# One kernel, one edit: the folded output weight as three rounded products, the sum of keys spread by two transfers, and the first attention tiles in another order

## The chip, the core and the metric

The kernel runs on one core of a Trainium2 chip. The core has engines that run side by side and meet at semaphores: TensorE (PE in the profile: matrix products and transposes), VectorE (DVE), ScalarE (ACT), GpSimd (POOL), and SyncE (SP), which here does nothing but issue the DMA transfers between device memory (DRAM) and on-chip memory (SBUF). Products end in accumulator banks (PSUM). Each engine runs its instructions in the order in which they were written down. The metric is device time in microseconds (us) of one execution; lower is better.

## The reference, cut to what matters

```python
x = A_x                                  # 2048 x 576
xn = _layernorm(x)
q, k, v = xn @ wqkv                      # 32 heads of 18
pq, pk = phi(q), phi(k)                  # phi(t) = (t + 1 if t > 0 else exp(t)) + 1e-6
kv = einsum("bhsd,bhse->bhde", pk, v)    # one 18 x 18 block a head
z = sum of pk over the tokens            # 576 numbers: the sum of keys
o = (pq @ kv) / (pq . z + 1e-6)
s = o @ wo
g = _silu(gelu(xn @ w1 + b1) @ w2 + b2)  # 576 -> 4608 -> 576
out = x + s * g
```

All inputs and the output are float32.

## The kernel before, in words

**Numbers in two halves.** TensorE takes two kinds of operand here: plain float32 (`F32`) and rounded float32 (`F32R`). Where the kernel uses the rounded kind it writes an operand `a` as `hi + lo`: `hi` is a rounded copy of `a`, made on ACT, and `lo` is `a - hi`, made on DVE (lines with `op=SUB`). A product is then three rounded products, hi*hi + hi*lo + lo*hi. The two halves of a weight are the tiles that end in `h` and `l`.

**Stages.** Tokens lie in 16 tiles of 128. Phase 1 goes through pairs of tiles. For each pair a Winograd-like scheme computes queries, keys and values (`products`, with steps 2, 1, e2, sa, 6, sb, e5, 7, 5, 4, 3 from `ORDER_X`; a number is a product with the weight pair `W_OF[number]`, and e2 and e5 are products with the last 64 rows of the weight). The accumulator banks `x0`, `xa` and `x1` hold three running results; `snapshot` (L900) copies `xa` to SBUF between products, since later sums need it as it stood. After each step a hook of the caller runs, and this is where everything else is put: the order of the whole phase is this hand-written order, engine by engine. Steps sa and sb are `state` (L473): 10 products that add the pair before to `ps_kva` and `ps_kvb`, the matrices kv of all heads with the sum of keys as one more row (row 126, `G`). The first two pairs are computed by `plain_x` without that scheme (L390 from `x00` to `x11`), and the first `state` stands between `x10` and `x12`.

For the last two pairs (tiles 12 to 15) the keys and values come first (part "kv"), and the queries after them (part "q"), once for pair 6 and once for pair 7. The hooks of these two query passes hold the end of the attention's preparation:

- `masked_state` copies the sum of keys out of PSUM (L1077, L1078) and the blocks on the diagonal of kv into `kvz` (`copy_predicated`, L1079 to L1081).
- `make_zb` spreads the sum of keys over all 128 partitions: a product with a matrix whose last row is ones (L1128), and a copy (L1132).
- `fold_wo` multiplies kv with the output weight: kw = kvz x wo, five groups of heads in six steps of two products (L1152), each copied from PSUM by ACT (L1159) or DVE (L1157), and moved to rows of another tile by DMA (L1163 to L1167). All of these products are plain float32.
- `by_sums` (POOL, L1101) multiplies phi(q) with the spread sum of keys, `denominators` (DVE, L1108 to L1112) adds up each head and inverts, `p_mult` (POOL, L1116) divides phi(q), and `pad` (ACT, L1123) fills the last columns.
- `split_kw` (ACT L1193, DVE or POOL L1194) makes the two halves of kw, and `store_kw` (L1197) stores it for later.

**The ten attention tiles.** `TO` lists ten of the tiles. For each, `transpose_p` turns phi(q) over on TensorE (5 transposes into `ptp`, L1252) and writes its halves `th` (ACT, L1256) and `tl` (DVE, L1257, L1258); `attend` multiplies them with kw into `ps_s` (28 products, L1287), copies the result (L1296) and stores it. While tile j is multiplied, tile j+2 is transposed and the sums of tiles j+4 and j+5 are made. `beside` puts other preparation for the feed-forward network between these tiles; among it is a sum of three terms on DVE (`sum_rest`, L534 to L538).

**The rest.** The feed-forward network follows (L1575, L1741), with the six other attention tiles spread through its second half. It takes four fifths of the time.

**Transfers.** All are issued by SP in the order of the program; each also waits until the one eight before it has landed.

Of the kernel before, what the change touches and what calls it, by code (L numbers as in the profile page):

```python
# [15 lines left out]
P = 128  # L16
# [31 lines left out]
def linear_attention_gated_ffn(ctx, tc, x, xT, wqkv, wo, w1, w1e, b1, w2, b2, out):  # L48
# [64 lines left out]
    zb_dram = dram.tile([P, D], F32, name="zb_dram")  # L113
# [51 lines left out]
    ORDER_X = (2, 1, "e2", "sa", 6, "sb", "e5", 7, 5, 4, 3)  # L165

# [19 lines left out]
    def q_tile(t):  # L186
        q_of[t] = tq.tile([P, D], F32, tag="q", name=f"q{t}", bufs=4)
# [237 lines left out]
    def phi_hi(key, src):  # L425

        e = e_of[key] = tq.tile([P, D], F32, tag="e", name=f"e{key}")
        nc.scalar.activation(as2(e), src, AF.Relu, scale=-1.0)
        nc.scalar.activation(e, e, AF.Exp, scale=-1.0)
        nc.scalar.activation(e, e, AF.Identity, bias=tiny[:, 0:1])  # L430

# [385 lines left out]
    k10 = phi_plain(2, x10)  # L817
    state(0)
    x12 = bank2("x12")
    plain_x(1, 1, 0, x12, THEN)  # L820
# [34 lines left out]
    def late_tiles(p):  # L855
        r_tile(p)
        f = R[p].rearrange("p a b -> p (a b)")
        if p == NPR:
            at = 0
            for n, cols in (("kvz", 640), ("sums_k", D), ("last_row", P), ("zb", D), ("mf", G)):  # L860
                late[n] = f[:, at : at + cols]
                at += cols
# [12 lines left out]
    def make_mask():  # L875
# [3 lines left out]
        nc.gpsimd.memset(late["sums_k"], 0.0)  # L879
        nc.gpsimd.memset(late["last_row"], 0.0)  # L880
        nc.gpsimd.affine_select(
            out=late["last_row"], in_=late["last_row"], compare_op=ALU.not_equal, fill=1.0,
            base=-G, pattern=[[0, P]], channel_multiplier=1,
        )
# [17 lines left out]
    def products(p, part, hooks, before=None):  # L902
# [8 lines left out]
        for i in ORDER_X:  # L911
# [57 lines left out]
    def phase1_pair(p):  # L969
# [8 lines left out]
        def h2():  # L978
# [7 lines left out]
            for n, t in enumerate(qp[::-1]):  # L986
                phi_q_hi(t)
# [3 lines left out]
        def h1():  # L991
            if early:
                rest_hi(prep), x_hi_ops(prep, 0, 14)
            for t in qp[::-1]:
                phi_q_max(t), store_q(t)
# [64 lines left out]
    for p in range(2, NPR):  # L1060
# [5 lines left out]
        2 * NPR - 3, 2 * NPR - 4, 2 * QH, 2 * QH + 1, 2 * NPR - 2, 2 * QH + 2, 2 * NPR - 1,  # L1066
# [3 lines left out]
    kvz, sums_k, last_row, zb_first = (late[n] for n in ("kvz", "sums_k", "last_row", "zb"))  # L1070
    wo_sb = late["wo"] + [k_bufs[0]]
    ln = GROUPS[-1][1]

    def masked_state():
        mask = late["mask"]
        nc.sync.dma_start(wo_sb[4][: GROUPS[4][1]], wo[GROUPS[4][0] :, :])
        nc.scalar.copy(sums_k[96 : G + 1, : 4 * G], ps_kv[0][96 : G + 1, : 4 * G])  # L1077
        nc.scalar.copy(sums_k[96 : G + 1, 4 * G :], ps_kv[1][96 : G + 1, :ln])  # L1078
# [4 lines left out]
    def first_phi():  # L1083
        phi_q_hi(TO[0]), phi_q_max(TO[0])
# [1150 lines left out]
```

## Time and profile before

| | us |
|---|---|
| Median of three runs (1088.2 to 1089.11) | 1088.75 |
| The profiled execution | 1088.02 |
| Its span, from first to last instruction | 1086.1 |
| PE busy in the span | 1075.6 (99%) |
| DVE, ACT, POOL busy | 819.6, 524.4, 535.2 |
| Query pass of pair 6 begins | 176.65 |
| First product of the spread and the fold (zb) | 187.43 |
| First transposes of the attention tiles | 202.36 |
| First product of the first attention tile | 203.85 |
| Feed-forward network begins | 247.49 |

The table gives the profiled execution's own time beside its span: 1.9 us lie outside the span, and the median of the runs lies 0.73 us above the profiled execution. Starts are counted from the span's start. A row of the timeline reads: start, duration, engine, line, operation, output and inputs, for products the size of the array's part and of the output, count, and in brackets the idle time of the engine just before and what ended it. The duration of one product includes its way through the array, so the distance between the starts of neighbouring products tells what one costs.

### The profile page before, as it was taken

Reading aid. Unit: us, or ns where it says so; the run is one execution under the profiler, and the core shown is the slowest. Engines: PE = TensorE matmul, PEld = TensorE weight load, DVE = VectorE, ACT = ScalarE, POOL = GpSimd, SP = SyncE. Lnnn points to the kernel's source line nnn. Section 1 sums busy time; section 2 is a strip of 40 time slices with the busy share of each in tenths; the row PEclk is TensorE's granted clock in tenths of the full one; section 3 lists DMA queues with packets and bytes.
Section 4 is the critical chain, followed back from the end, with each engine's and each line's share of the span. In section 5 each row is a group of like instructions: output and inputs, shape, how many; then the busy total and the mean of one; then the engine's idle time right before and its main releaser. Section 6 shows DMA issues by size and latency. Waiting matters only on the chain.

```text
span 1086.1 us, 17916 instructions
## 1 busy us (share of the span) xinstructions
PE 1075.6 (99%) x6492; PEld 990.6 (91%) x6492; DVE 819.6 (75%) x1197; ACT 524.4 (48%) x872; POOL 535.2 (49%) x555
## 2 busy tenths in 40 slices
PE   9999999999999999999999999999999999999998
PEld 8999999898988989989899898998989899998988
DVE  7997853787898988989889886575847566574856
ACT  7656655645454554544545445253443444242442
POOL 3133141576596776866867754143433525242340
PEclk9999999999999999999999999999999999999999
DMA  6678634699567585685765797886767657666653
GB/s 240 195 290 226 219 127 147 224 378 378 195 248 274 215 299 202 226 302 197 288 245 205 267 393 288 288 302 216 224 198 238 213 180 244 201 228 226 215 156 130
DMA packets 91120, 258.63 MB, mean 238 GB/s; under 512 B 12182, under 2 KB 25494, under 8 KB 88728
## 3 DMA queue, kind: packets, MB, share of 16 engines
q1 hardware_dynamic: 91032, 257.49, 68.8%
q8 instruction: 51, 0.84, 0.3%
q14 instruction: 37, 0.30, 0.1%
HBM read 155.16 MB, written 101.40 MB: 236 GB/s over the span
## 4 chain that ended last, share of the span: by engine, by line
PE 94%; ACT 2%; DMA 1%; DVE 1%; issue 1%; POOL 1%; SPq 0%; POOLq 0%; ACTq 0%; DVEq 0%
PE pm L1741 35%; PE a L1575 11%; PE zy L1575 11%; PE e L1575 11%; PE b L1575 5%; PE xaall L390 4%; PE x L390 3%; PE pd L1862 2%; PE x1all L390 2%; PE psa L1287 2%; PE ps_s L1287 1%; PE ps_kva L473 1%; PE x0all L390 1%; PE xakv L390 1%; DMA s_dram<-s 1%
## 5 line engine op out<-in xcount | busy, mean ns | idle before, releaser
L1678 POOL TENSOR_TENSOR g<-g 128x256 f32<-128x256 f32 x204 | 185.6, 938 | 56.5 <-DVE h_l L1329 49.5
L1747 DVE TENSOR_TENSOR macc<-pm,macc 128x576 f32<-128x576 f32 x218 | 163.9, 752 | 44.0 <-PE pm L1741 43.1
L1326 ACT CAST h_h<-g 128x512 fp32r<-128x512 f32 x204 | 122.7, 621 | 117.4 <-PE pm L1741 116.4
L1329 DVE TENSOR_TENSOR h_l<-g,h_h 128x512 fp32r<-128x512 f32 x204 | 165.2, 816 | 2.3 <-ACT h_h L1326 2.3
L1575 PE MATMUL a<-X,wa 128*128 128x512 f32 x432 | 110.1, 390 | 0.0
L1575 PEld LDWEIGHTS a<-X,wa 128*128 128x128 f32 x432 | 79.7, 188 | 15.3
L1592 ACT COPY mid<-a 128x512 f32<-128x512 f32 x36 | 21.1, 585 | 111.2 <-PE a L1575 111.2
L1678 POOL TENSOR_TENSOR mid<-g 128x256 f32<-128x256 f32 x68 | 52.0, 784 | 45.6 <-ACT g L1583 44.5
L1595 DVE TENSOR_TENSOR mid<-b,mid 128x512 f32<-128x512 f32 x36 | 24.8, 689 | 61.4 <-PE b L1575 61.3
L1377 POOL TENSOR_TENSOR w1raw<-w1raw 128x256 f32<-128x256 f32 x18 | 13.3, 740 | 90.6 <-ACT h_h L1326 47.7
L1583 ACT ACTIVATE g<-b,b1c 128x512 f32<-128x512 f32 x36 | 24.8, 689 | 66.9 <-DVE b L1601 66.8
L1575 PE MATMUL e<-X,wc 128*128 128x512 f32 x216 | 55.4, 392 | 0.0
L1575 PE MATMUL zy<-X,wd 128*128 128x512 f32 x216 | 54.9, 389 | 0.0
L1575 PE MATMUL e<-X,wd 128*128 128x512 f32 x216 | 54.8, 389 | 0.0
L1575 PE MATMUL zy<-X,wc 128*128 128x512 f32 x216 | 54.8, 389 | 0.0
L274 POOL TENSOR_TENSOR R<-R,bc 128x640 f32<-128x640 f32 x9 | 15.8, 1770 | 70.4 <-DMA R<-xT 47.1
L1575 PEld LDWEIGHTS zy<-X,wd 128*128 128x128 f32 x216 | 40.5, 188 | 8.6
L1575 PEld LDWEIGHTS zy<-X,wc 128*128 128x128 f32 x216 | 40.5, 188 | 8.4
L1575 PEld LDWEIGHTS e<-X,wd 128*128 128x128 f32 x216 | 40.5, 188 | 8.4
L1575 PEld LDWEIGHTS e<-X,wc 128*128 128x128 f32 x216 | 40.1, 188 | 8.1
L1583 ACT ACTIVATE g<-e,b1c 128x512 f32<-128x512 f32 x36 | 24.8, 689 | 45.3 <-DVE e L1608 45.3
L1994 POOL TENSOR_TENSOR qa<-qa,dena 128x576 f32<-128x576 f32 x6 | 7.0, 1168 | 62.5 <-issue 56.6
(1019 smaller groups left out, 3234.6 us busy)
## 6 DMA issues: line engine op xcount, KB each, us to landing
we<-we_dram SPq DMA_DIRECT2D x72, 224.0 KB
w2raw<-w SPq DMA_DIRECT2D x10, 1152.0 KB
x_dram<-X SPq DMA_DIRECT2D x6, 1792.0 KB
w1raw<-w SPq DMA_DIRECT2D x18, 512.0 KB
op_a<-wa SPq DMA_DIRECT2D x18, 512.0 KB
op_c<-wc SPq DMA_DIRECT2D x18, 512.0 KB
op_d<-wd SPq DMA_DIRECT2D x18, 512.0 KB
wc<-op_c SPq DMA_DIRECT2D x18, 512.0 KB
```

What stands on the lines that cost most here:

```text
L390: nc.tensor.matmul(dst, st, w, start=start, stop=stop, skip_group_check=True)
L1287: nc.tensor.matmul(ps[:, h, :HD], st[:, k, :], w[v][k][:, h * HD : (h + 1) * HD], start=(i == 0), stop=(i == len(seq) - 1),)
L1326: nc.scalar.copy(pair[0], src)
L1329: eng.tensor_tensor(pair[1], src, pair[0].bitcast(F32), op=SUB)
L1575: nc.tensor.matmul(ps, st, mv, start=first and n == 0, stop=n == len(seq) - 1, skip_group_check=True,)
L1583: nc.scalar.activation(g, ps, AF.Gelu_apprx_tanh, bias=b1c[:, f : f + 1])
L1592: nc.scalar.copy(m1_sb, A)
L1595: tt(u1_sb, B, m1_sb, op=ADD)
L1678: nc.gpsimd.tensor_tensor(dst[:, cs], a[:, cs], b[:, cs], op=op)
L1741: nc.tensor.matmul(ps[:, q, :HD], hs[p][st][:, cs], m[:, p, :], start=(n == 0 and i not in CHAIN), stop=(n == 5), skip_group_check=True,)
L1747: nc.vector.tensor_tensor(dst, src, dst, op=ADD)
L1862: nc.tensor.matmul(ps, st[:, cs], w_all.rearrange("p n d -> p (n d)")[:, w], start=(i == 0), stop=(i == len(seq) - 1),)
```

## The change

- **Fold.** The weights of the fold are split: `wo_hi` and `wo_lo` write the halves of the five pieces of wo into places of weight tiles whose key and value columns are no longer needed (`kv_columns` of T2, T3, T4), and `state_hi` and `state_lo` write the halves of kvz. Each product of the fold becomes three rounded ones. The last groups are copied from PSUM by ACT alone. The fold begins after step 1 of the last query pass, where it began after step 2.
- **Sum of keys.** `make_zb` goes. The row is stored to DRAM (`z_dram`, 576 numbers) and loaded again into all 128 partitions (`sum_of_keys`). The later copy for the second half is loaded from the same row, and the store of the whole spread tile goes.
- **Order.** Tiles 8 and 9 become the first attention tiles; their queries are loaded into the places of wo (`load_early_q`). In both query passes e2 comes before product 1 (`ORDER_Q`). The first transposes come before step 3 of the last query pass. Sums on POOL, `split_kw`, the third step of `sum_rest` and the first `state` change places; within an attention tile the 28 products go through `th` with the high half, `tl`, and `th` with the low half.

On PE at the end of phase 1 (`x0q`, `xaq` and `x1q` are the banks of the last query pass, `ps_kw` those of the fold), before:

```order
L390 MATMUL x0q_1974<-wB21h,X 128x288
L1128 MATMUL zb_1981<-R_1542 128x288
L1128 MATMUL zb_1984<-R_1542 128x288
L1152 MATMUL ps_kw_1989<-R_1718,R_1542 126x288
L1152 MATMUL ps_kw_1992<-R_1718,R_1542 126x288
L390 MATMUL xaq_1995<-wB11h,X 128x288
L390 MATMUL xaq_1995<-wB11l,X 128x288
L390 MATMUL xaq_1995<-wB11h,X 128x288 x2
```

On PE at the same place, now:

```order
L392 MATMUL x0q_1988<-wRh,XR_1571 128x288
L392 MATMUL x0q_1988<-wRl,XR_1571 128x288
L392 MATMUL xaq_1999<-wB11h,X 128x288
L392 MATMUL xaq_1999<-wB11l,X 128x288
L392 MATMUL xaq_1999<-wB11h,X 128x288 x2
L392 MATMUL xaq_1999<-wB11l,X 128x288
L392 MATMUL xaq_1999<-wB11h,X 128x288
L1201 MATMUL ps_kw_2009<-X,wT4h 126x288 x2
L1201 MATMUL ps_kw_2009<-X,wT4l 126x288
L1201 MATMUL ps_kw_2014<-X,wT4h 126x288 x2
L1201 MATMUL ps_kw_2014<-X,wT4l 126x288
```

The two products of the spread are gone, the fold stands behind product 1, and one product of it is three.

On SP from the end of the state to the fold's first moves (`kph` and `R` take the last piece of wo, `weo` are halves of another weight, `zb` is the spread sum, `b1c` a bias), before:

```order
L1076 DMA kph_134<-wo 72x576
L592 DMA we_dram<-weo_1926 128x1792
L1092 DMA b1c<-b 128x36
L1163 DMA kw_1987<-kw_1987 2x576
L1166 DMA kr_2012<-kw_1987 112x576
```

On SP at the same place, now:

```order
L1104 DMA R_1542<-wo 72x576
L1119 DMA z_dram<-R_1542 1x576
L1114 DMA zb<-z_dram 128x576
L1101 DMA R_1713<-q_dram 128x576 x2
L601 DMA we_dram<-weo_1908 128x1792
L1149 DMA b1c<-b 128x36
L1212 DMA kw_2007<-kw_2007 2x576
```

The store of the row, the load that spreads it and two loads of queries now stand ahead of the store of `weo` and of the fold's moves.

On DVE in the middle of the attention tiles (`wa_rest0ef` is the sum of three terms), before:

```order
L536 SCALAR_TENSOR_TENSOR wa_rest0ef<-wa_rest0gm,sgn,wa_rest0ef 64x512
L538 TENSOR_TENSOR wa_rest0ef<-wa_rest0ef,wa_rest0gm 32x512
L1257 TENSOR_TENSOR tl_2485<-ptp_2478,th_2484 128x512
L1258 TENSOR_TENSOR th_2484<-ptp_2478,th_2484 64x128
L1108 TENSOR_REDUCE den_2492<-bs_2437 128x32
```

On DVE at the same place, now:

```order
L545 SCALAR_TENSOR_TENSOR wa_rest0ef<-wa_rest0gm,sgn,wa_rest0ef 64x512
L1322 TENSOR_TENSOR tl_2509<-ptp_2502,th_2508 128x512
L1323 TENSOR_TENSOR th_2508<-ptp_2502,th_2508 64x128
L547 TENSOR_TENSOR wa_rest0ef<-wa_rest0ef,wa_rest0gm 32x512
L1165 TENSOR_REDUCE den_2517<-bs_2462 128x32
```

The third step of the sum has moved behind the halves of a transposed tile.

The diff, cut to its core:

```diff
-    zb_dram = dram.tile([P, D], F32, name="zb_dram")
+    z_dram = dram.tile([1, D], F32, name="z_dram")
...
     ORDER_X = (2, 1, "e2", "sa", 6, "sb", "e5", 7, 5, 4, 3)
+    ORDER_Q = (2, "e2", 1, "sa", 6, "sb", "e5", 7, 5, 4, 3)
...
-    state(0)
     x12 = bank2("x12")
-    plain_x(1, 1, 0, x12, THEN)
+    plain_x(1, 1, 0, x12, THEN[:6], last=False)
+    state(0)
+    plain_x(1, 1, 0, x12, THEN[6:], first=False)
...
             if p == NPR - 2:
-                rest_lo(prep), x_lo_ops(prep, 0, 8), x_lo_ops(prep, 8, 14)
+                x_lo_ops(prep, 8, 14), rest_lo(prep), x_lo_ops(prep, 0, 8)
...
     TO = [
-        2 * NPR - 3, 2 * NPR - 4, 2 * QH, 2 * QH + 1, 2 * NPR - 2, 2 * QH + 2, 2 * NPR - 1,
+        2 * QH, 2 * QH + 1, 2 * NPR - 3, 2 * NPR - 4, 2 * NPR - 2, 2 * QH + 2, 2 * NPR - 1,
...
+    def wo_hi(i):
+        nc.scalar.copy(wo_ops[i][0], wo_src[i])
+
+    def wo_lo(i):
+        h, l = wo_ops[i]
+        nc.vector.tensor_tensor(l, wo_src[i], h.bitcast(F32), op=SUB)
+
+    def sum_of_keys(dst):
+        nc.sync.dma_start(dst, bass.AP(tensor=z_dram.tensor, offset=z_dram.offset, ap=[[0, P], [1, D]]))
+
+    def state_sums():
+        nc.scalar.copy(sums_k[96 : G + 1, : 4 * G], ps_kv[0][96 : G + 1, : 4 * G])
+        nc.scalar.copy(sums_k[96 : G + 1, 4 * G :], ps_kv[1][96 : G + 1, :ln])
+        nc.sync.dma_start(z_dram, sums_k[G : G + 1])
+        zb.append(tw.tile([P, D], F32, tag="raw", name="zb", bufs=1))
+        sum_of_keys(zb[0])
...
     products(NPR - 2, "q", {
-        1: round_sums, "sb": lambda: (masked_state(), round_hi()), 7: lambda: (round_lo(), round_store()),
-        4: first_phi,
+        2: load_last_wo,
+        "e2": lambda: (round_sums(), wo_hi(0), wo_hi(1), wo_lo(0), wo_lo(1)),
+        "sa": lambda: (round_hi(), round_lo(), wo_hi(2), wo_lo(2)),
+        "sb": state_sums,
+        "e5": lambda: (masked_state(), load_early_q(0), load_early_q(1), wo_hi(3)),
+        7: lambda: (state_hi(), wo_hi(4), wo_lo(3)),
+        5: lambda: (state_lo(), wo_lo(4), round_store()),
+        4: lambda: phi_q_hi(TO[2]),
     }, NPR - 1)
...
-                nc.tensor.matmul(
-                    ps, kvz[:rows, at : at + n], wo_sb[i][:rows, hs], start=True, stop=True
-                )
+                for m, (v, w) in enumerate(((0, 0), (0, 1), (1, 0))):
+                    nc.tensor.matmul(
+                        ps, kvz_at(v, rows, at, n), wo_ops[i][w][:, h], start=m == 0, stop=m == 2
+                    )
                 dst = kw[i][:n, hs] if n < P else kr4[:, hs]
-                if h:
+                if h and i < 3:
                     nc.vector.tensor_copy(dst, ps)
...
-    products(NPR - 1, "q", {2: f2, 1: f1, 6: f6, 7: f7, 5: f5, 4: f4})
+    products(NPR - 1, "q", {
+        2: f2, 1: f1, "sa": fsa, 6: f6, "e5": fe5, 7: f7, 5: f5, 4: f4,
+    })
...
-        seq = []
-        for k in range(4):
-            seq += [(th, 0, k), (th, 1, k), (tl, 0, k)]
+        seq = [(st, v, k) for st, v in ((th, 0), (tl, 0), (th, 1)) for k in range(4)]
         seq += [(th, 0, 4), (th, 1, 4)]
...
-        1: ((0, "split", 0),), 2: ((0, "sums", 0),), 3: ((0, "sums", 1), (0, "sums", 2)),
+        1: ((0, "split", 0),), 2: ((0, "sums", 0),), 3: ((0, "sums", 1),),
...
+        if j == 4:
+            rests[0].sums(2)
...
-        if 0 < j < NA - 5:
+        if 1 < j < NA - 5:
             by_sums(j + 5)
         if j + 4 < NA:
             denominators(j + 4)
             p_mult(j + 4)
+        if j < 2:
+            by_sums(j + 5)
```

More of the change, by code (lines that the diff above doesn't have):

```diff
@@ L993, in h1 @@
                 rest_hi(prep), x_hi_ops(prep, 0, 14)
-            for t in qp[::-1]:
+            for n, t in enumerate(qp[::-1]):
+                if n and not early:
+                    phi_q_hi(t)
                 phi_q_max(t), store_q(t)
@@ L1248, in transpose_p @@
     def transpose_p(j):
-        pb = p_bufs[j % len(p_bufs)]
-        pt = bank2(f"ptp{j}").rearrange("p a b -> p (a b)")
-        for k in range(KT):
-            nc.tensor.transpose(pt[:, k * P : (k + 1) * P], pb[:, k * P : (k + 1) * P], ident)
+        if j not in ptps:
+            transpose_only(j)
+        pt = ptps.pop(j)
         th = thp.tile([P, KT, P], F32R, tag="th", name=f"th{j}")
@@ L1261, in linear_attention_gated_ffn @@
     transpose_p(0)
+    split_kw(1, dve)
+    split_kw(2, dve)
     split_kw(3, pool)
     store_kw(3)
-    p_bufs.append(tw.tile([P, KT * P], F32, tag="op", name="pbuf"))
-    denominators(2), p_mult(2)
     split_kw(4, dve)
```

119 lines of the change are left out of this document (70 added, 49 removed).

## The prediction, made before the changed kernel ran

> **What bounds the kernel now.** I read the page's engine rows first, then PE's own waits, then the timeline wherever one of those waits falls, on PE and on the engine named.
>
> ```profile
> span 1086.1 us, 17916 instructions
> PE 1075.6 (99%) x6492; PEld 990.6 (91%) x6492; DVE 819.6 (75%) x1197; ACT 524.4 (48%) x872; POOL 535.2 (49%) x555
> ```
>
> ```profile
> PE ps_kw L1152 <- ACT kw L1159: 0.5, 1, 0.5
> PE xaq L390 <- ACT u L900: 0.5, 1, 0.5
> PE ps_kva L473 <- ACT R L689: 0.4, 1, 0.4
> PE x0kv L390 <- DVE X L299: 0.3, 1, 0.3
> ```
>
> TensorE is the bound: busy 99% of the span. A change can pay in two ways, by less work on PE or by filling PE's few holes, which in the second fence (us in total, times, longest) are short and single. These holes lie in the first 250 us, where this change works. The feed-forward network behind shows no such wait of PE, so what reaches it earlier should end earlier.
>
> **The change part by part.** The time of each hole is read between starts on PE, less what the products before it need.
>
> *The first state moved into x12.*
>
> ```profile
> 37.61 0.55 PE L390 MATMUL x<-wRl,XR 128*128 128x432 f32 x2
> 38.61 1.12 PE L473 MATMUL ps_kva<-kph,vb 128*127 128x126 f32 x8 [0.45 <-ACT R L689]
> ...
> 36.51 0.59 ACT L671 CAST X<-pt3a 128x512 fp32r<-128x512 f32 x1 [3.38 <-PE pt3a L661]
> ```
>
> A product of 432 columns costs 0.20 (0.133 for 288, below, by the columns), so x10 ends near 38.0 and the state stands until 38.61. Now 12 products of x12 stand between, 2.4 us, and ACT's copies that the state waits for are done long before. What x12 needs first, the cast of L671, ended at 37.10, before PE comes to it. Gain 0.55; I leave 0.05 for the hand-over.
>
> *The halves of x in another order.*
>
> ```profile
> 160.89 0.42 PE L390 MATMUL x0kv<-wB21l,X 128*128 128x288 f32 x2
> 161.61 0.81 PE L390 MATMUL x0kv<-wB21h,X 128*128 128x288 f32 x4 [0.30 <-DVE X L299]
> ...
> 159.46 2.10 DVE L299 TENSOR_TENSOR X<-R,X 128x1024 fp32r<-128x1024 f32 x2
> ```
>
> Two products of 288 columns cost 0.27, so 0.45 of the 0.72 is a hole. DVE makes the part that this product needs as the second of the two, which end at 161.56. Put first, it takes its share of the 2.10 (768 of 1792 columns, 0.9) from 159.46 at the latest and ends before 160.4, ahead of the product's turn at 161.16. The other parts end no later than 161.6 and are wanted by later steps. Gain 0.45.
>
> *Query pass of pair 6.*
>
> ```profile
> 177.31 0.30 PE L390 MATMUL x0q<-wB21h,X 128*128 128x288 f32 x1
> 177.76 0.40 PE L390 MATMUL xaq<-wB11h,X 128*128 128x288 f32 x1 [0.15 <-DVE kph L433]
> ...
> 183.67 0.29 PE L390 MATMUL x1q<-wT1h,X 128*128 128x288 f32 x1
> 184.42 0.40 PE L390 MATMUL xaq<-wT4h,X 128*128 128x288 f32 x1 [0.46 <-ACT u L900]
> ...
> 182.52 0.73 DVE L1079 COPY_PREDICATED R<-mask,ps_kva 126x504 f32<-126x504 uint8 x1 [4.09 <-ACT R L1077]
> 183.42 0.44 DVE L458 TENSOR_TENSOR q<-x0q,u 128x288 f32<-128x288 f32 x1
> ...
> 183.97 0.40 ACT L900 COPY u<-xaq 128x288 f32<-128x288 f32 x1 [0.40 <-PE x1q L390]
> ```
>
> At 177.76 the hole is 0.45 less one product (0.13), 0.32; the two products of e2 that now come first fill 0.27 of it. At 184.42 it is 0.62: the snapshot may not overwrite `u` before DVE has added it to x0q, and that addition stood behind `masked_state`. Now it stands ahead, so the snapshot can follow product 7 at once and ends as product 5 does. New here, off PE's path: on ACT the casts of wo and kvz (five and two), on DVE as many subtractions. I price each like the largest of its size shown, a DVE subtraction of 576 columns at 0.75 (last fence below). Laid end to end among what ACT and DVE do there already, ACT has done the last cast near 184.7 and DVE the half of kvz near 185, while PE comes to the fold near 187.5. That cover is 2.5 us. Gain 0.27 + 0.6 = 0.87.
>
> *Spread and fold.*
>
> ```profile
> 186.64 0.30 PE L390 MATMUL x0q<-wB21h,X 128*128 128x288 f32 x1
> ...
> 190.63 1.14 PE L1152 MATMUL ps_kw<-R,R 126*126 126x288 f32 x4
> ...
> 191.73 0.30 PE L390 MATMUL x0q<-wRl,XR 128*128 128x288 f32 x1
> 191.87 0.97 PE L390 MATMUL xaq<-X 128*128 128x288 f32 x6
> 192.67 1.13 PE L1152 MATMUL ps_kw<-R,R 126*126 126x288 f32 x4
> ...
> 202.36 1.25 PE L1252 MATMUL ptp<-ident,vb 128*128 128x128 f32 x10
> 203.85 0.53 PE L1287 MATMUL ps_s<-kw_h,th 128*128 128x288 f32 x2 [0.23 <-ACT th L1256]
> ...
> 208.53 0.52 PE L1287 MATMUL ps_s<-kw_h,th 128*128 128x288 f32 x2
> ```
>
> From 186.64 to 203.85 are 17.21 us. A rounded product takes 0.133 (six from 191.87 to 192.67). A plain one is two records: from 190.63 to 191.73 lie two plain products and one rounded, so (1.10 - 0.13) / 2 = 0.48 each. The stretch holds 50 rounded (6.65), 14 plain (6.8) and ten transposes (1.1): 14.5, and 2.7 of holes. Afterwards: 50 + 36 rounded products, 11.4, and the same transposes, 12.5. The holes that I find with the new order: the fold's second group waits for ACT's copy of its first bank, since ACT is still in phi of tile 13 and the snapshot (0.47), and the first attention tile waits for the cast of its transposed tile (0.15). All other copies are ready, since product 6, 7, 5 or 4 stands between the groups. With 0.2 for hand-overs the stretch is 13.3. Gain 3.9, of which 2.0 is work and 1.9 holes.
>
> The spread no longer costs PE anything, and it costs SP two transfers in series. The row leaves PSUM near 182.4; nearest rows for what follows:
>
> ```profile
> SPq L256 <- DMA st_dram<-mv: 20.1, 6, 7.5
> ```
>
> ```profile
> 171.13 0.38 SPq L575 DMA_DIRECT2D we<-w1e  x1
> ```
>
> ```profile
> 176.17 1.84 POOL L581 TENSOR_TENSOR we<-we 128x128 f32<-128x128 f32 x4 [12.90 <-DMA we<-w1e]
> ```
>
> A like pair, a small store and a load that spreads it, made SP wait 3.4 on average (20.1 in 6) and 7.5 at most. A load of 256 KB that POOL waited for took 5.0 (171.13 to 176.17). With 3.4 + 5.0 the sum of keys is spread near 190.8; SP has little else in flight here, so I expect it earlier. TensorE needs it, through sums, denominators and `p_mult`, at its first transpose near 196.6. Worked back (three sums of 1.4, `p_mult` 1.2 and `pad` 0.3 in a row), it has to be there by 190.9. A gain it cannot bring beyond the two products already counted, as PE would wait for no spread even before; the longest rows (7.5 + 5.0, so 194.9) would cost 4.0. I take nothing, since the means just fit, and keep 4.0 for the slow end.
>
> Behind the spread on SP stand two loads of queries and the store of `weo`; ACT's copy of the fold's fourth group goes into that store's buffer. Issued near 187 and with the same 5.0 it is free at 192, and ACT comes at 193. The cover is 1 us; a longer store stops PE by what it exceeds that.
>
> *The attention tiles.*
>
> ```profile
> 220.87 0.42 PE L1287 MATMUL ps_s<-kw_l,th 128*128 128x288 f32 x2
> 221.58 0.77 PE L1252 MATMUL ptp<-ident,pbuf 128*128 128x128 f32 x5 [0.28 <-POOL pbuf L1116]
> ...
> 230.18 0.71 PE L1252 MATMUL ptp<-ident,vb 128*128 128x128 f32 x5
> 231.16 0.50 PE L1287 MATMUL ps_s<-kw_h,th 128*128 128x288 f32 x2 [0.27 <-DVE th L1258]
> ```
>
> ```profile
> 228.44 1.54 DVE L538 TENSOR_TENSOR wa_rest0ef<-wa_rest0ef,wa_rest0gm 32x512 f32<-32x512 f32 x1
> ```
>
> ```profile
> 199.59 1.40 POOL L1101 TENSOR_TENSOR bs<-q,zb 128x576 f32<-128x576 f32 x1
> ```
>
> ```profile
> 200.41 1.20 DVE L1194 TENSOR_TENSOR kw_l<-kw,kw_h 128x576 fp32r<-128x576 f32 x1
> 201.53 0.75 DVE L1194 TENSOR_TENSOR kw_l<-kr,kw_h 128x576 fp32r<-128x576 f32 x1
> ```
>
> Two holes of 0.44 each: 221.58 less 221.14, where POOL makes a later sum before this tile's `p_mult`, and 231.16 less 230.72, where DVE's third step of 1.54 stands ahead of `th`. Both are put the other way round, with 1 us and more of room then. The first tile (208.53 less 203.85, 4.68) takes 4.45 (28 products 3.7, the transposes 0.5, 0.2 for ACT's casts of kw) when `tl` and the low half of kw come later in the row. Gain 0.88 + 0.23 = 1.1. The transfers keep up: the loads in this stretch begin when SP has stored kw, and that moves forward by as much as PE does.
>
> *What I take off.* A DVE subtraction beside a POOL sum took 1.20, one without 0.75 (last three rows). The sums on POOL now lie in the middle of the fold: 0.3 for this and for restarts.
>
> **Sum.** 0.55 + 0.45 + 0.87 + 3.9 + 1.1 - 0.3 = 6.6. The profiled execution took 1088.02 (span 1086.1 and 1.9 around it), so 1081.4; the median of the runs shown is 0.73 above it, so 1082.2.
>
> **The rivals.**
>
> *Copies set the pace of the fold.* Each of its groups needs both PSUM banks emptied, and ACT has nine copies where it had six. If every one of the other five steps waits 0.4 (about what the wait for `ACT kw` in the second fence was), 2.0 are lost: 1084.2. Against it: the products between the groups, 0.8 to 1.1 us each.
>
> *POOL holds DVE up.* The subtraction of 200.41 began while the POOL sum of 199.59 ran and ended at 201.61, that is 0.62 after the sum did, like one that had waited for it. As a mechanism here: three DVE operations that PE waits for (phi of tiles 13 and 12, the first low half of kw) could each stand behind a whole POOL sum of 1.4. That is 4.2 if all of it reaches PE, in place of the 0.3: 1086.1. Against it: by my working only one of the three starts while POOL works. [...]
>
> *Rounded products are no cheaper.* If each of the 36 cost what one record of a plain product does (0.24), the fold would be 8.6 against 6.8, a gain of 2.0 turned into a loss of 1.8, and 1086.0. Against it: the rounded products between the groups, on the same 288 columns, at 0.133.
>
> *Slower: the spread arrives too late.* Everything that SP issues, and each POOL sum, stands behind the second transfer. For each us after 190.9 PE waits one us at its first transpose. To end slower by 0.2% (2.2 us, about what a measurement of this kernel can tell from no change) it has to arrive at 190.9 + 6.6 + 2.2 = 199.7, 17.3 us after the row left PSUM; with 20 us the loss is 11.5 against a gain of 6.6, and the time 1093.6. For it: the row is read 128 times from one place, and no row shows that for 288 KB. Against it: the longest rows add up to 12.5, which gives 1086.2.
>
> **How the numbers follow.** Forecast 0.70 (its own range 1080.9 to 1083.5); copies 0.10, 1084.2; POOL 0.05, 1086.1; rounded products 0.02, 1086.0; late spread, slower, 0.06; no named cause, with the gain eaten in the feed-forward network, 0.07, of which I give 0.04 to no change and 0.03 to slower. The low end is the sum without the 0.3 and with the small holes that stay between attention tiles gone (208.53 to 247.49 is 38.96; nine tiles of 28 products at 0.133 and seven times five transposes at 0.107 are 37.2; less the 0.88 already taken, 0.9 is left): 1081.0, and I say 1080.8. The high end takes in the copies and part of POOL's hold: 1085.2. Faster by over 0.2% is below 1086.6: 0.70 + 0.10 + 0.05 + 0.02 = 0.87; same 0.04; slower 0.06 + 0.03 = 0.09.
>
> **What would show it.** In the changed profile PE should have no hole before `ps_kva` near 38, none at the third product of x0kv, and none before product 4 of the query pass; the fold should be 36 records spaced 0.13; the first attention tile should begin near 198.0 (203.85 less the first four terms, 5.8); the network should begin near 240.9 (247.49 less 6.6), and keep its length. PE rows `ps_kw <- ACT kw` with more than 1 us in total speak for the copies; `ptp <- POOL vb` for the late spread; DVE rows of 1.2 and more under `phi_max` for POOL. Wrong I would be if the network begins early and the end does not follow.

## The result and the profile after

The changed kernel takes 1082.63 us (median of four runs, 1082.16 to 1082.9) against 1088.83 for the kernel before (four runs, 1088.2 to 1089.11): a ratio of 0.9943, with a 95% interval of 0.9926 to 0.9961. On another chip the same kernel gave 0.9955 (0.9941 to 0.9968). The forecast was 1082.2. Every ratio below with an interval is against the kernel before on the chip of that run; two executions of the kernel with a third transfer took 1508 us at a granted clock of 0.65 and are left out of its ratio.

The engine rows of the page, and PE's own waits, of the changed kernel:

```profile
span 1081.2 us, 17934 instructions
...
PE 1071.6 (99%) x6500; PEld 990.3 (92%) x6500; DVE 827.0 (76%) x1201; ACT 528.5 (49%) x879; POOL 535.8 (50%) x552
```

```profile
PE x L392 <- ACT wB11h L343: 1.3, 2, 0.8
PE ps_s L1350 <- POOL kw_l L1245: 0.7, 1, 0.7
...
PE ps_s L1350 <- DVE q L467: 0.2, 1, 0.2
...
PE ps_kw L1201 <- ACT kw L1208: 0.2, 1, 0.2
```

The waits that the prediction started from (`ps_kva`, `xaq`, `x0kv`) are gone, and the one on the copies of the fold has gone from 0.5 to 0.2. A new one is the longest of this stage: the first attention tile waits for a low half of kw that POOL makes. The first row is the landing of the first weights; it lies ahead of everything that was changed, and the section on what was not expected comes back to it.

The places of the prediction, in the timeline of PE of the changed kernel:

```profile
40.56 0.55 PE L392 MATMUL x<-wB21l,X 128*128 128x432 f32 x2
40.95 0.82 PE L482 MATMUL ps_kva<-kph,vb 128*127 128x126 f32 x6
...
160.54 0.43 PE L392 MATMUL x0kv<-wB21h,X 128*128 128x288 f32 x2
160.80 0.43 PE L392 MATMUL x0kv<-wB21l,X 128*128 128x288 f32 x2
161.06 0.70 PE L392 MATMUL x0kv<-wB21h,X 128*128 128x288 f32 x4
...
176.16 0.29 PE L392 MATMUL x0q<-wB21h,X 128*128 128x288 f32 x1
...
185.26 0.30 PE L392 MATMUL x0q<-wB21h,X 128*128 128x288 f32 x1
...
188.26 0.53 PE L1201 MATMUL ps_kw<-X,wT4h 126*126 126x288 f32 x2 [0.18 <-ACT kw L1208]
...
198.55 1.69 PE L1350 MATMUL ps_s<-kw_h,th 128*128 128x288 f32 x8 [0.20 <-DVE q L467]
```

The state follows its predecessor at once (40.95 after 40.56), and x0kv runs without a hole. From the last query pass (185.26) to the first attention tile (198.55) there are 13.29 us, where there were 17.21.

The next fence has the first attention tile itself, on PE, then what stands on DVE, ACT and POOL in the same 6.5 us:

```profile
202.02 0.53 PE L1350 MATMUL ps_s<-kw_l,th 128*128 128x288 f32 x2 [0.19 <-DVE kw_l L1245]
203.28 0.53 PE L1350 MATMUL ps_s<-kw_l,th 128*128 128x288 f32 x2 [0.74 <-POOL kw_l L1245]
...
205.02 1.29 PE L1350 MATMUL ps_s<-kw_h,th 128*128 128x288 f32 x8
...
199.56 2.40 DVE L1245 TENSOR_TENSOR kw_l<-kr,kw_h 128x576 fp32r<-128x576 f32 x2
201.88 1.96 DVE L1245 TENSOR_TENSOR kw_l<-kw,kw_h 128x576 fp32r<-128x576 f32 x1
...
198.99 0.67 ACT L1244 CAST kw_h<-kr 128x576 fp32r<-128x576 f32 x1 [0.37 <-DMA kr<-kw]
...
199.97 1.38 POOL L1173 TENSOR_TENSOR pbuf<-q,den 128x576 f32<-128x576 f32 x1 [3.75 <-DMA kw_dram<-kw]
201.31 1.92 POOL L1245 TENSOR_TENSOR kw_l<-kr,kw_h 128x576 fp32r<-128x576 f32 x1
203.20 1.93 POOL L1158 TENSOR_TENSOR bs<-q,zb 128x576 f32<-128x576 f32 x1
```

The tile takes 6.47 us (198.55 to 205.02), where it took 4.68. Three low halves on DVE take 4.3 us in place of the 2.25 that the 0.75 of the prediction's row makes, and POOL's three operations stand beside them without a gap. ACT's cast of kw 3 waits 0.37 for rows that a DMA moves.

POOL had a low half, the third product and a sum in this tile before the change too. What has moved in are halves of DVE's. DVE and POOL before:

```profile
202.57 0.74 DVE L1194 TENSOR_TENSOR kw_l<-kr,kw_h 128x576 fp32r<-128x576 f32 x1
206.24 0.69 DVE L1194 TENSOR_TENSOR kw_l<-kw,kw_h 128x576 fp32r<-128x576 f32 x1
...
204.45 1.44 POOL L1194 TENSOR_TENSOR kw_l<-kr,kw_h 128x576 fp32r<-128x576 f32 x1 [3.46 <-ACT kw_h L1193]
206.40 1.55 POOL L1116 TENSOR_TENSOR pbuf<-q,den 128x576 f32<-128x576 f32 x1 [0.51 <-DVE den L1112]
```

There DVE had made three of its four halves when the tile began (203.85), and one was left; now three are made in the tile.

From start to start, the whole account of the two profiles (us; the network is counted to the end of the span):

| stretch | before | after | gained | forecast |
|---|---|---|---|---|
| start to the transposes near 36 | 35.88 | 36.45 | -0.57 | 0 |
| to x0kv of pair 6 (first state) | 124.74 | 124.09 | 0.65 | 0.55 |
| to its query pass (halves of x) | 16.03 | 15.62 | 0.41 | 0.45 |
| to the last query pass | 9.99 | 9.10 | 0.89 | 0.87 |
| to the first attention tile (spread, fold) | 17.21 | 13.29 | 3.92 | 3.9 |
| first attention tile | 4.68 | 6.47 | -1.79 | 0.23 |
| the other nine, to the network | 38.96 | 37.71 | 1.25 | 0.88 |
| network | 838.61 | 838.47 | 0.14 | 0 |

The prediction took off 0.3 for POOL beside DVE and placed it in the fold; the fold came out as forecast, and the loss stands in the first attention tile. The span fell by 4.9; the medians fell by 6.2, since the profiled run of the changed kernel is the slowest of its four and that of the kernel before the fastest of its own.

### The profile page after: what moved, and what is told of

It reads as the page before. It is cut to its first block, busy times and chain, and to the rows that moved or that the text cites. A ratio compares the mean times of both kernels' runs of the same rounds, so it can differ in the third digit from the quotient of the medians.

```text
span 1081.2 us, 17934 instructions
## 1 busy us (share of the span) xinstructions
PE 1071.6 (99%) x6500; PEld 990.3 (92%) x6500; DVE 827.0 (76%) x1201; ACT 528.5 (49%) x879; POOL 535.8 (50%) x552
## 4 chain that ended last, share of the span: by engine, by line
PE 97%; ACT 1%; DMA 1%; POOL 1%; issue 0%; DVE 0%; SPq 0%; POOLq 0%; DVEq 0%
PE pm L1805 35%; PE a L1639 11%; PE zy L1639 11%; PE e L1639 11%; PE b L1639 5%; PE xaall L392 4%; PE x L392 4%; PE ps_s L1350 3%; PE pd L1926 2%; PE x1all L392 2%; PE psa L1350 2%; PE ps_kva L482 1%; PE xakv L392 1%; PE x0all L392 1%; PE x1kv L392 1%; PE xaq L392 0%
## 5 line engine op out<-in xcount | busy, mean ns | idle before, releaser
L1440 POOL TENSOR_TENSOR w1raw<-w1raw 128x256 f32<-128x256 f32 x18 | 13.3, 740 | 91.9 <-ACT h_h L1389 47.7
```

## The experiments

Two quantities are read from every run's timeline: the first attention tile (first product to first product of the second tile), and the stretch from there to the network.

| kernel | first tile | to the network | attention in all |
|---|---|---|---|
| before | 4.68 | 38.96 | 43.64 |
| before, second profile | 4.77 | 38.67 | 43.44 |
| changed | 6.47 | 37.71 | 44.18 |
| changed, second profile | 6.49 | 37.74 | 44.23 |
| third product behind kw 3 | 6.50 | 37.70 | 44.20 |
| low half of kw 3 on DVE | 7.13 | 37.45 | 44.58 |
| POOL kept out | 5.03 | 38.24 | 43.27 |
| POOL kept out, sum 7 later | 5.34 | 38.43 | 43.77 |
| POOL kept out, old orders | 5.07 | 38.23 | 43.30 |
| old orders of attention | 6.50 | 37.87 | 44.37 |
| plain products and spread on TensorE | 7.67 | 38.09 | 45.76 |
| third transfer | 6.61 | 37.45 | 44.06 |
| early orders back | 6.48 | 37.72 | 44.20 |

**Why the first tile is long: two misses.** The first theory was POOL's queue: `pbuf` lies in a buffer that a store of kw must leave first, and the low half of kw 3 stood behind its product.

```diff
-        p_bufs.append(tw.tile([P, KT * P], F32, tag="op", name="pbuf"))
...
-        denominators(2), p_mult(2)
+        denominators(2)
...
     store_kw(4)
+    p_bufs.append(tw.tile([P, KT * P], F32, tag="op", name="pbuf"))
+    p_mult(2)
```

> The changed kernel with the buffer and the product of the third query tile (pbuf) made on POOL behind the low half of kw 3 again, in place of ahead of it; its denominators stay where they are. Theory: the first attention tile took 6.47 us (198.55 to 205.02) where 4.45 was forecast, because POOL's product waited 3.75 us for the store of kw that frees its buffer and the low half of kw 3 stood behind it. Then here that low half runs from about 199.7, the hole before the product that reads it (0.9) is gone, and the one before it (0.35) stays: first tile 5.2 to 5.7 us, network start 0.8 to 1.2 us earlier, time 1081.6 (0.999 of the changed kernel). Rival: the landing of kw 3 and DVE's halves beside POOL set it, whatever POOL does first: first tile 6.2 to 6.5, network start and time unchanged.

Measured: 0.9956 of the kernel before (0.9943 to 0.9968), first tile 6.50. DVE and POOL of this run:

```profile
199.59 2.67 DVE L1245 TENSOR_TENSOR kw_l<-kr,kw_h 128x576 fp32r<-128x576 f32 x2
202.19 1.72 DVE L1245 TENSOR_TENSOR kw_l<-kw,kw_h 128x576 fp32r<-128x576 f32 x1
...
199.77 1.89 POOL L1245 TENSOR_TENSOR kw_l<-kr,kw_h 128x576 fp32r<-128x576 f32 x1 [3.51 <-ACT kw_h L1244]
201.62 1.68 POOL L1173 TENSOR_TENSOR pbuf<-q,den 128x576 f32<-128x576 f32 x1
```

POOL now makes kw 3 first, as meant, and DVE's own halves come as much later: the last is there at 203.9, as in the changed kernel. The order on POOL is not the cause; the rival named for this run had it right. The second run took POOL's share of kw away:

```diff
-    split_kw(3, pool)
+    split_kw(3, dve)
```

> The changed kernel with the low half of kw 3 made on DVE in place of POOL. Theory (POOL's wait is the cause): DVE makes three low halves in a row from 199.56 and is held up by POOL's product of 1.4 us once, so the low half of kw 3 is there at 202.5 to 203.0 in place of 203.2 and kw 4 at 203.3 to 203.7: first tile 5.7 to 6.3 us, network start 0.2 to 0.8 us earlier. Rival (DVE beside POOL is the cause: two low halves took 2.40 us there, one 1.96): with nothing of POOL's but one product beside them the four low halves take 3.0 to 3.4 us in a row, and the first tile falls to 5.0 to 5.6 us.

Measured: 0.9961 (0.9949 to 0.9974), first tile 7.13, longer than either theory had it.

```profile
199.90 4.28 DVE L1245 TENSOR_TENSOR kw_l<-kr,kw_h 128x576 fp32r<-128x576 f32 x3
204.10 0.74 DVE L1245 TENSOR_TENSOR kw_l<-kw,kw_h 128x576 fp32r<-128x576 f32 x1
...
200.06 1.62 POOL L1173 TENSOR_TENSOR pbuf<-q,den 128x576 f32<-128x576 f32 x1 [3.51 <-DVE th L1323]
201.64 1.92 POOL L1158 TENSOR_TENSOR bs<-q,zb 128x576 f32<-128x576 f32 x1
```

While POOL's two operations run, to 203.56, DVE gets through fewer than three halves; after them one takes 0.74. So the two engines run at each other's cost. Nearly clear of each other the four halves take 2.85 us and the two POOL operations 2.98 (rows of the next run), 5.83 together; here both were done in 4.94 (199.90 to 204.84), nearer to the sum than to the longer of the two.

**POOL kept out of the tile.** With the third product in a part of the fold's own buffer that is free earlier, its sum's inverse and the fourth tile's sum earlier, and all halves on DVE:

```diff
-        p_bufs.append(tw.tile([P, KT * P], F32, tag="op", name="pbuf"))
+        p_bufs.append(kw_all[0].rearrange("p a b -> p (a b)")[:, D : D + KT * P])
...
+        denominators(2)
         split_kw(0, dve)
...
-        denominators(2), p_mult(2)
+        p_mult(2), by_sums(3)
...
-    split_kw(3, pool)
+    split_kw(3, dve)
```

> The changed kernel with POOL kept out of the first attention tile: pbuf lies in the part of the folded weight's buffer whose rows have been moved (so its product needs no store of kw), the third tile's denominators stand ahead of the first low half of kw, the fourth tile's sum stands behind the third's product, and all low halves of kw are made on DVE. Theory now, after the two runs before: in the first tile DVE and POOL run at each other's cost, whatever stands first; from 199.5 they have 3.0 us of DVE work for kw and 4 to 5 us of POOL work, and the low halves are there only when most of both is done. With POOL's work done before 199.2, DVE's low halves take 0.75 each, the last is there near 202.2, and the first tile's last bound is the landing of kw 3 (its cast ends at 199.7). First tile 4.5 to 5.0 us in place of 6.47, network start 1.2 to 1.8 us earlier, time 0.9986 of the changed kernel. Rival: DVE alone is too slow for four low halves and the two of the transposed tile, POOL or not: first tile 5.8 us or more, time unchanged.

> The changed kernel itself once more, on the same chip as the three below, as their base, and as a second look at the first 36 us. Every theory expects its ratio to the kernel before near 0.994 and its first attention tile at 6.3 to 6.6 us. If the 0.57 us that it was late at 36 us in the first profile (36.45 against 35.88) come from the start of one execution and not from the change, this execution may begin anywhere between 35.9 and 36.6, and it keeps the 4.5 to 5.0 us from there to the network as it was.

Measured on one chip: 1081.9 us, 0.9943 (0.9929 to 0.9956), against 1083.4, 0.9955 (0.9941 to 0.9968), for the changed kernel: 1.5 us or 0.9986, though the two intervals overlap. DVE and POOL with POOL kept out, and a wait of PE's:

```profile
199.37 2.18 DVE L1248 TENSOR_TENSOR kw_l<-kr,kw_h 128x576 fp32r<-128x576 f32 x3
201.47 0.75 DVE L1248 TENSOR_TENSOR kw_l<-kw,kw_h 128x576 fp32r<-128x576 f32 x1
...
196.65 1.55 POOL L1173 TENSOR_TENSOR kw<-q,den 128x576 f32<-128x576 f32 x1 [0.51 <-DVE den L1169]
198.16 1.43 POOL L1158 TENSOR_TENSOR bs<-q,zb 128x576 f32<-128x576 f32 x1
...
199.59 0.53 PE L1353 MATMUL ps_s<-kw_h,th 128*128 128x288 f32 x2 [0.19 <-ACT kw_h L1247]
```

Four halves in 2.85 us, and a first tile of 5.03 in place of 6.49: the theory's mechanism holds, just above its 4.5 to 5.0. What the tile still has over the forecast 4.45 is 0.58; PE waited in it for ACT's cast of kw 3 (last row). Of the 1.46, a third came back, so that by the timelines 0.96 is left from the last query pass to the network (57.44 to 56.48), less than the 1.2 to 1.8 expected. It came back as a single hole at the seventh tile's transposes, where POOL's sum runs beside a DVE step of the denominators (0.18 at 204.07, where POOL stands still, 1.37 here) and PE's transposes wait for the product behind it:

```profile
217.22 1.37 DVE L1168 TENSOR_SCALAR den<-den 128x32 f32<-128x32 f32 x1
...
217.13 1.42 POOL L1158 TENSOR_TENSOR bs<-q,zb 128x576 f32<-128x576 f32 x1 [0.73 <-DMA q<-q_dram]
...
220.65 0.77 PE L1298 MATMUL ptp<-ident,vb 128*128 128x128 f32 x5 [0.49 <-POOL vb L1173]
```

So the sum was put behind the product (`2 < j` and `j < 3` in the loop over the tiles):

> The kernel with POOL kept out of the first tile (the run before), and the sum for tile 7 behind the product for tile 6 on POOL in place of ahead of it. There 0.5 us of the 1.44 that the first tile gained were lost again at one place: the transposes of the seventh tile stood until 220.65 for POOL's product, which waited for denominators on DVE, and those had one small step of 1.37 us beside the sum that came with a late load of queries. Theory: with the sum behind, that wait goes, the other tiles stay, and from the last query pass to the network there are 56.0 us in place of 56.5 (57.4 in the changed kernel): time 0.9987 of the changed kernel's. Rival: the tiles are paced by POOL and DVE as a whole, so the wait moves to a later tile: 56.4 or more.

Measured: 56.95 us from the last query pass to the network, 0.9948 (0.9936 to 0.9961), so no better. The wait moved on, as the rival had it; PE now stood before the products of the eighth tile, and the first tile varied by 0.3:

```profile
229.67 1.29 PE L1353 MATMUL ps_s<-kw_h,th 128*128 128x288 f32 x8 [0.52 <-DVE th L1327]
```

**Do the named orders of the attention tiles matter?** The old orders were put back in the changed kernel, and then with POOL kept out:

```diff
-        seq = [(st, v, k) for st, v in ((th, 0), (tl, 0), (th, 1)) for k in range(4)]
+        seq = []
+        for k in range(4):
+            seq += [(th, 0, k), (th, 1, k), (tl, 0, k)]
...
-        1: ((0, "split", 0),), 2: ((0, "sums", 0),), 3: ((0, "sums", 1),),
+        1: ((0, "split", 0),), 2: ((0, "sums", 0),), 3: ((0, "sums", 1), (0, "sums", 2)),
...
-        if 1 < j < NA - 5:
+        if 0 < j < NA - 5:
```

> The changed kernel with the attention tiles in the old order: tl interleaved with the low half of kw, the third sum of the rest beside tile 3, and the sum for tile 6 ahead of the product for tile 5 on POOL. Theory: the two single holes of 0.44 come back (tile periods of 4.7 and 4.8 in place of 4.3), so from the second tile to the network 38.5 to 38.8 us in place of 37.7; the first tile is unchanged (6.3 to 6.7), since its last low half sets it in either order of products. Rival: the order of products is what the later tiles gained from, and only it: every period grows by 0.1, and no single hole shows.

> The kernel with POOL kept out of the first tile, with the attention tiles in the old order (products, sums on POOL, third sum of the rest). In the changed kernel the old orders had cost nothing from the second tile on. Theory: that was because the first tile held PE up for 2 us, in which POOL and DVE got ahead; with the first tile short the old orders cost again what they cost in the kernel before: single holes of 0.4 to 0.9 at the seventh and the ninth tile, and from the second tile's first product to the network 38.7 to 39.3 us (37.7 in the changed kernel, 38.2 with POOL kept out). The first tile takes 5.2 to 5.8, since tl and the low halves are wanted earlier. Rival: the old orders cost nothing at any time, and the holes of the kernel before came from something else: 38.3 or less.

The holes that these two call those of the seventh and ninth tile are the prediction's, near 221 and near 231. Both theories missed. In the changed kernel the old orders cost 0.13 us from the second tile on (37.87 against 37.74), with no single hole; with POOL kept out they cost nothing (38.23 against 38.24, with the hole near 220 in both), and the first tile took 5.07 where 5.2 to 5.8 was expected. The times are 0.9955 (0.9939 to 0.9971) and 0.9951 (0.9936 to 0.9966). So the later tiles did not gain by the orders that the prediction named. What the table shows instead is that a long first tile goes with a short rest: 7.13 with 37.45, 6.5 to 6.6 with 37.45 to 37.9, 5.0 to 5.3 with 38.2 to 38.4, 4.7 with 38.7 to 39.0. (The 38.09 behind 7.67 holds a second tile of 4.90, where the changed kernel has 4.26, run in part at a granted clock of 0.55, last section.) A reading that fits is that PE comes later, POOL and DVE get ahead, and fewer of their products are late. It was not tested by itself, and the order of the tiles (`TO`) with the places of their loads was never put back, so the cause of the 1.25 stays open; that the named orders are not the cause by themselves is shown.

> The kernel before once more, for a second profile. Every theory expects its holes at the places that the prediction named (0.5 to 0.6 at the first state, x0kv, product 4 of the query pass, the seventh and the ninth tile), 211 to 212 us from the transposes near 36 to the network, and a start of those transposes anywhere between 35.6 and 36.9, which is what the runs so far have shown.

The second profile of the kernel before took 1087.4 us. From the transposes near 36 to the network it has 211.41 us (211.61 in the first profile), with the hole near 221 again, but 0.13 near 231 in place of 0.44: of the two 0.44, the prediction counted one that does not show in every execution.

**Work and order in the fold.** With plain products and the spread on TensorE, in the new order:

```diff
-                for m, (v, w) in enumerate(((0, 0), (0, 1), (1, 0))):
-                    nc.tensor.matmul(
-                        ps, kvz_at(v, rows, at, n), wo_ops[i][w][:, h], start=m == 0, stop=m == 2
-                    )
+                nc.tensor.matmul(
+                    ps, kvz_at(0, rows, at, n).bitcast(F32), wo_ops[i][0][:, h].bitcast(F32),
+                    start=True, stop=True,
+                )
...
-        sum_of_keys(zb[0])
...
     def f2():
+        make_zb()
```

> The changed kernel in its own order of work, with the fold as 12 plain products (of the high halves alone, so the low halves are left out of the folded weight) in place of 36 rounded ones, and with the sum of keys spread by two plain products and two ACT copies in place of the second transfer. Theory: of the 3.9 us that the spread and the fold gained, 2.0 are work (14 plain products at 0.48 are 6.7, 36 rounded ones at 0.13 are 4.8) and the rest is order. Then the stretch from product 2 of the last query pass to the first attention tile is 13.3 + 1.9 = 15.2 us, and the time 1.9 us more than the changed kernel's (1.0018 of it). Rival: the order alone brought the gain and the copies set the pace of the fold, so the plain products fill waits that are there anyway: stretch below 14.0 us, time within 0.7 us of the changed kernel's.

Measured: 15.43 us for the stretch (184.75 to 200.18), 2.1 more than 13.29: the theory. The time is 0.9982 (0.9973 to 0.9991), 2.9 us above the changed kernel's by the ratios (0.9955, taken on another chip), where 1.9 was expected; the timeline has lost 1.6 more in the attention tiles (45.76 against 44.2), where PE waited twice for low halves of kw in the first tile and then ran at a granted clock of 0.55 (last section).

**The slack of the spread.**

```diff
-        sum_of_keys(zb[0])
+        sum_of_keys(z2_dram)
+        nc.sync.dma_start(zb[0], z2_dram)
```

> The changed kernel with a third transfer in the spread: the row is spread into a DRAM tile of 288 KB first, and that is loaded. Theory: the spread ends a few us before TensorE needs it (the first sum on POOL began at 188.99 and waited for the queries, not for the spread; the first transposes at 196.04 waited for nothing, their last input having ended at 195.49). A transfer of 4 to 6 us more moves the first sum to 192 to 194 and the first transposes by what exceeds 0.5 us: 2.5 to 4.5 us more time than the changed kernel, with a wait of PE at the transposes on the product that POOL makes. Rival: the queries behind it and POOL's row of sums have the slack of another transfer: time within 0.7 us of the changed kernel's, no wait of PE at the first transposes.

Measured: 0.9989 (0.9979 to 0.9999), and 16.77 us for the stretch, 3.48 more. The size is the theory's, the place is another: POOL's first sum began at 191.08, no transposes waited for it, and PE stood in the fold.

```profile
192.95 0.30 PE L393 MATMUL x1q<-wT1h,X 128*128 128x288 f32 x1
195.11 0.29 PE L1203 MATMUL ps_kw<-wT4h,wT1h 72*8 72x288 f32 x1 [1.86 <-ACT kw L1210]
...
187.94 0.43 SPq L602 DMA_DIRECT2D we_dram<-weo  x1
...
194.66 0.70 ACT L1210 COPY kw<-ps_kw 126x288 f32<-126x288 f32 x2 [2.55 <-DMA we_dram<-weo]
...
191.08 2.81 POOL L1160 TENSOR_TENSOR bs<-R,zb 128x576 f32<-128x576 f32 x2 [13.74 <-DMA R<-q_dram]
```

The store of `weo` stood behind the third transfer (187.94, where it was 184.43), and ACT's copy of the fold's fourth group waited for its buffer until 194.6. If the store takes the same 6.7 us from issue in the changed kernel (an estimate from these two rows), the buffer is free there at 191.1, 1.3 before ACT comes at 192.40. So the late spread did its harm here through the transfers queued behind it before the sums felt it.

**The early orders.** First state, halves of x, product 1 ahead of e2, and masked copies, all put back at once, since they lie at different places:

```diff
-    plain_x(1, 1, 0, x12, THEN[:6], last=False)
     state(0)
-    plain_x(1, 1, 0, x12, THEN[6:], first=False)
+    plain_x(1, 1, 0, x12, THEN)
...
-                x_lo_ops(prep, 8, 14), rest_lo(prep), x_lo_ops(prep, 0, 8)
+                rest_lo(prep), x_lo_ops(prep, 0, 8), x_lo_ops(prep, 8, 14)
...
-    ORDER_Q = (2, "e2", 1, "sa", 6, "sb", "e5", 7, 5, 4, 3)
+    ORDER_Q = (2, 1, "e2", "sa", 6, "sb", "e5", 7, 5, 4, 3)
```

> The changed kernel with the first state back ahead of x12, the halves of x in the old order, product 1 ahead of e2 in the query passes, and the masked copies of the state back ahead of the phi steps. Theory: each loses at its own place what the prediction gave it. From the transposes near 36 to x0kv of pair 6 0.55 us more (124.1 to 124.6), from there to its query pass 0.4 more (15.6 to 16.0), from there to the last query pass 0.9 more (9.1 to 10.0); what follows as it was, so 1.9 us more time. Rival: the gaps are elastic and a later step gives some of it back: under 1.0 us in all.

Measured: 124.74, 16.01 and 10.42 us for the three stretches, that is 0.65, 0.39 and 1.32 more, 2.36 in all, and 0.9972 (0.9963 to 0.9981), or 1.8 us above the changed kernel on the same chip. The first two are as expected. The third is 0.4 above it and above the kernel before (9.99): product 4 waits 0.81 for the snapshot of `u` where it waited 0.46. The snapshot may not overwrite `u` before DVE has added it to x0q, and in the order of this kernel that addition stands behind the masked copies, as before the change, and behind a subtraction of wo too.

```profile
184.58 0.40 PE L392 MATMUL xaq<-wT4h,X 128*128 128x288 f32 x1 [0.81 <-ACT u L903]
```

## Why the prediction was right, and where not

- *First state, halves of x, query pass of pair 6:* 0.55, 0.45 and 0.87 were forecast, 0.65, 0.41 and 0.89 measured, and putting the orders back lost 0.65, 0.39 and 1.32 again. Shown; the third lost more than it had gained, which by the order on DVE goes to the subtractions of wo that stand there now.
- *Spread and fold:* 13.3 us forecast, 13.29 measured. The hole at the fold's second group was there, 0.35 where 0.47 stood (the last product before 188.26 began at 187.78, and one takes 0.13), and the start of the attention waited 0.4, not 0.15. The plain work put back took 2.1 us of the 3.9, where 2.0 were called work. That the other 1.8 came from holes is read from the timelines alone. The rival that copies set the pace falls with it: `ps_kw <- ACT kw` is 0.2 in all, and the plain products were not hidden. The rival that rounded products are no cheaper falls too: they came 0.13 apart in the fold (193.39, 193.52).
- *Spread on SP:* in time: POOL's first sum began at 188.99, ahead of the 190.9 by which the sum of keys had to be there. The cover of the `weo` buffer, called 1 us, is 1.3 by an estimate from the run with the third transfer, and it is what breaks first. A rival of slower by a late spread had the right queue, and its price for each us lacked the 1.4 us that the products took longer behind the hole there, at a granted clock of 0.53 (last section).
- *The attention tiles* are the step that failed. "The first tile takes 4.45" came to 6.47: a loss of 1.79 in place of a gain of 0.23. The prediction looked for POOL beside DVE in the fold ("only one of the three starts while POOL works"; two did, the phi of 190.06 and the first low half of 195.37, at 0.99 and 1.46 us, and the fold was on time even so). It did not look in the first tile, where the change makes three of DVE's low halves next to POOL's low half, product and sum, and put that at nothing; it took 0.3 off in all, and the tile alone missed by 2.0. Keeping POOL out gave 1.44 to 1.46 of that back; the other 0.58 is in part the wait for the cast of kw 3. The rival "POOL holds DVE up" named the two engines, at another place: three halves took 2.18 us with POOL nearly clear of them, and 4.28 beside two POOL operations. That a DVE operation waits for the whole of one of POOL's, as that rival had it, was not shown.
- *The two single holes* "put the other way round" gained 1.25 by the account, against 0.88; but with the old orders back the gain stayed, so the reason given for it was wrong, and the cause stays open. First tile and later tiles together lost 0.54 where 0.8 to 1.1 was to be gained.
- *Sum:* 6.6 were forecast; from 36 us on, the profiles show 5.5. The network began at 242.73 where 240.9 was forecast; 0.57 of that lie in the first 36 us. The forecast of 1082.2 came out close to 1082.63 with this error of 1.1 in it, because the medians of the first comparison lie 6.2 apart; on the other chip they lie 4.35 apart (1087.75 and 1083.4). That the time came out within 0.5 us is luck; the early stretches and the fold are not.

## What to carry to other kernels

When an order brings DVE subtractions like the low halves of kw next to products and sums on POOL, count both as nearly one queue: ask for the sum (4.94 us here, for 2.85 and 2.98 nearly clear of each other), not for which comes first. A hole that is closed can in part come back at a later place (1.46 us gained in the first tile, 0.5 of it lost at the seventh tile's transposes). A reason that fits the size of a gain is not yet its cause: the orders that were to bring 0.88 us could be undone for 0.13.

## What was not expected of the hardware

**A hole of 2 us, and 1.4 us more behind it.** In the run with the third transfer PE stood from 193.08 to 195.11; the next products came 0.13 us apart, as ever, and from 195.59 on 13 of them 0.24 apart, until 198.7. The windows view gives each stretch with busy times, then the granted clock (PEclk), the DMA share and GB/s. Of the run with the third transfer:

```profile
195.20:198.70 3.50, 3.50 (x16) 3.06 (x16) 1.91 (x5) 1.89 (x6) 2.29 (x3) 0.53 0.31 93
198.70:202.00 3.30, 3.21 (x25) 3.00 (x25) 1.58 (x5) 3.07 (x8) 1.17 (x1) 0.99 0.91 339
```

Of the run with plain products, where two holes of 1.3 and 0.8 us stand close together:

```profile
206.30:209.60 3.30, 3.30 (x15) 3.28 (x16) 3.15 (x7) 1.33 (x2) 0.79 (x1) 0.55 0.98 316
```

Of the run with the low half of kw 3 on DVE, behind a single hole of 1.35 us:

```profile
204.20:207.00 2.80, 2.73 (x18) 2.41 (x19) 2.65 (x6) 1.24 (x2) 0.00 (x0) 1.00 0.84 232
```

The granted clock was 0.53 and 0.55 for some 3.3 us in the first two, and 1.00 after the hole of the third; in the first that cost 1.4 us (13 products at 0.24 in place of 0.13). After a hole of 1.66 us near 9 us (last fence) the next six products took 1.29 us (9.42 to 10.71), as they did in the first profile of the changed kernel after a hole of 0.50 (8.46 to 9.75). So a slow stretch followed one hole of 2.0 us and two of 1.3 and 0.8, and none followed single holes of 1.35 and 1.66; what decides between them was not shown.

**The first 36 us differ from one execution to the next.** Over thirteen profiles of eleven kernels, all alike there, the transposes near 36 began between 35.62 and 36.89 us. The one in which they began last, a second profile of the changed kernel:

```profile
8.46 0.91 ACT L343 CAST wB11h<-raw 128x864 fp32r<-128x864 f32 x1 [1.41 <-DMA raw<-wqkv]
...
9.42 1.45 PE L392 MATMUL x<-wB11h,X 128*128 128x432 f32 x6 [1.66 <-ACT wB11h L343]
```

These weights landed later there (the same cast began at 6.90 in the first profile of the kernel before), and PE waited for them. The 0.57 us by which the changed kernel's first profile was late at 36 us lie within this spread and need be no part of the change. So the span of one execution is no measure for half a microsecond; distances between two later places of one timeline are a better one.
